# Partial sums of a first half kept in DRAM instead of SBUF, with more buffers for a stream of weights

## The chip, the cores and the metric

One core of a Trainium2 chip runs the whole program. The metric is the device time of one execution in microseconds (us). The kernel before takes 1258.06 us, the median of three runs (1256.82 to 1258.31). The execution that the profiler recorded took 1256.72 us; its instructions span 1254.9 us.

## The reference

Attention with normalised queries and keys, then a layer with squared ReLU, then a gated pair of products:

```python
q_n, k_n = rmsnorm(q, g_q), rmsnorm(k, g_k)          # 4 x 12 heads, 448 x 64
attn = softmax(q_n @ k_n.T / 8);  x = attn @ v       # -> 1792 tokens x 768
r = np.maximum(x @ w_in, 0.0);  x = (r * r) @ w_out  # 768 -> 2048 -> 768
h = (x @ w1) * (x @ w2) @ w3;   y = h @ w_out2       # 768 -> 1024 -> 1024 -> 768
```

The weights come as 64-bit floats, `q`, `k` and `v` as 32-bit ones.

## The kernel before

**Work and batches.** The four batches of 448 tokens follow one another. While the attention of batch b+1 runs head by head (the loop over `h`, lines 663 to 697), the matrix products of batch b fill the gaps of TensorE (PE): `fill(n)` draws pieces of three matmuls from a generator, six times a head. During batch 0 the filler is the product of `w3` and the second `w_out`, formed once (`gen_w3o`, to about 195 us). Then come the products of batch 0 (`gen_moe(0)`, about 195 to 511 us, beside heads 14 to 25), batch 1 (to about 780), batch 2 (to about 1046), and batch 3 with no attention beside it. A product is split in high and low parts, so each block of weights takes three matmuls (L258 to L260).

**The stream of weights.** Weights come in numbered units of 128 x 384 or 128 x 512 numbers. For batch 0 of `w_in`, `w_out`, `w1` and `w2` (88 units) a unit is 64-bit, and its way has many stations: a load by SP's queue into a `raw64` tile (L178); two passes that make 32-bit words in place (L192 on ScalarE, L197 on GpSimd or L195 on ScalarE); a *join* on VectorE (DVE, L204) into a `raw` tile; a store of that to DRAM for the later batches (L212); the high part copied into an `hl` tile (L104, ScalarE) and the low part subtracted into it (L112, mostly GpSimd). For batches 1 to 3 the unit is loaded as 32-bit straight into a `raw` tile (L181). There are 4 `raw64`, 4 `raw` and 4 `hl` tiles. `advance(u)`, called when unit u is used, issues the loads up to u+2+5 (64-bit) or u+2+3 (32-bit), words to u+2+3, joins to u+2+2, the low parts to u+2.

**Tiles of the products.** `relu2` (L324) uses an `r` and a `gf` tile: ReLU, its square, the product of PSUM and `r`, and the low part. The second product of each layer sums over 2048 rows in two halves: `keep` copies the sums of the first half into six `acc` tiles, `add` (L342) adds the second half to them. Results leave through `osb` tiles.

**Attention's last step.** `stage_v` puts the sums of two heads into `xf` (L617, DVE). `stage_x`, called in the next iteration, transposes the norms on PE (L598) into the only tile of the pool `ps_kv`, and DVE multiplies (L623). `stage_k` and `stage_v` use the same PSUM tile.

**What sets the order.** Each engine and each DMA queue works in order. The order is set at build time by a scheduler that follows the program's order, dependences and free tiles.

Of the kernel before, what the change touches and what calls it, by code (L numbers as in the profile page):

```python
# [29 lines left out]
def attention_moe_kernel(  # L30
# [15 lines left out]
    nc = tc.nc  # L46
    B, P, H, C, D = q_nat.shape
# [20 lines left out]
    VLO_ENG = "gvgv"  # L68


    SPLIT_AHEAD = 2
    HI_AHEAD = 1
    JOIN_AHEAD = 2
    WORD_AHEAD = 3
    LOAD32_AHEAD = 3
    LOAD64_AHEAD = 5

    const = ctx.enter_context(tc.tile_pool(name="const", bufs=1))
    xp = ctx.enter_context(tc.tile_pool(name="x", bufs=8))
    actp = ctx.enter_context(tc.tile_pool(name="act", bufs=8))  # L80
    x2p = ctx.enter_context(tc.tile_pool(name="x2", bufs=6))
    accp = ctx.enter_context(tc.tile_pool(name="acc", bufs=6))
    rawp = ctx.enter_context(tc.tile_pool(name="raw", bufs=4))
    hlp = ctx.enter_context(tc.tile_pool(name="hl", bufs=4))
    t2 = ctx.enter_context(tc.tile_pool(name="t2", bufs=2))
    t1 = ctx.enter_context(tc.tile_pool(name="t1", bufs=1))
    t3 = ctx.enter_context(tc.tile_pool(name="t3", bufs=3))
# [4 lines left out]
    ps_kv = ctx.enter_context(tc.tile_pool(name="ps_kv", bufs=1, space=bass.MemoryType.PSUM))  # L92
    ps_mm = ctx.enter_context(tc.tile_pool(name="ps_mm", bufs=3, space=bass.MemoryType.PSUM))

    w3o = dram.tile([2 * NE, 128, 512], F32, name="w3o")

    ident = const.tile([P, P], F32, name="ident")
# [12 lines left out]
    def sub_on(eng, out, in0, in1):  # L110
        e = nc.vector if eng == "v" else nc.gpsimd
        e.tensor_tensor(out=out, in0=in0, in1=in1, op=ALU.subtract)  # L112
# [59 lines left out]
    def load_next():  # L172
        i = pos["load"]
        src = units[i][0]
        n = src.shape[-1]
        if is64(i):
            t = t3.tile([128, 512, 2], U32, name="raw64", tag="raw64", bufs=4)
            nc.sync.dma_start(out=t[:, :n, :], in_=src.bitcast(U32).rearrange("p (n t) -> p n t", t=2))  # L178
        else:
            t = rawp.tile([128, 512], F32, name="raw", tag="raw")  # L180
            nc.sync.dma_start(out=t[:, :n], in_=src)  # L181
        raws[i] = t
        pos["load"] += 1
# [68 lines left out]
    def use(u):  # L252
        advance(u)
        return hls.pop(u).rearrange("p a (k m) -> p a k m", m=128)

    def mm3(ps, w, wk, x, i, n):
        last = n - 1
        nc.tensor.matmul(ps, w[:, 0, wk, :], x[0], start=(i == 0), stop=False)  # L258
        nc.tensor.matmul(ps, w[:, 0, wk, :], x[1], start=False, stop=False)  # L259
        nc.tensor.matmul(ps, w[:, 1, wk, :], x[0], start=False, stop=(i == last))  # L260
# [7 lines left out]
    def gen_w3o():  # L268
        for ic in range(NIC):
            ws = None  # L270
            for half in range(2):
                ps = ps_mm.tile([128, 512], F32, name="mm", tag="mm")
                for jc in range(NIC):
                    if ws is None or jc * 2 // NIC >= len(ws):
                        ws = (ws or []) + [use(w3_at[2 * ic + len(ws or [])])]
                    if ic == 0:
                        advance(wo_at[half, jc])
                        wo[half, jc] = hls.pop(wo_at[half, jc])
                    w = ws[jc * 2 // NIC]
                    mm3(ps[:, :HC], w, jc % (NIC // 2), hl_pair(wo[half, jc], HC), jc, NIC)  # L280
                    yield 3
                o = t2.tile([128, S], F32, name="osb", tag="osb")
                copy_on("a", o[:, :HC], ps[:, :HC])
                k, c = divmod(ic, NIC // 2)
                nc.sync.dma_start(
                    out=w3o.rearrange("(e k) p (c m) -> e k p c m", k=2, m=128)[half * 3:half * 3 + 3, k, :, c, :]
                    .rearrange("e p m -> p e m"),
                    in_=o[:, :HC].rearrange("p (e m) -> p e m", m=128),
                )
# [26 lines left out]
    def gen_moe(b):  # L316
        u = U0 + b * (2 * NFC + 4 * NE + 4 * NJ + 2 * NE)
        x = [xs.pop((b, i)) for i in range(KX)]
        acc = [None] * NE
        x2 = [None] * NE  # L320
        for half in range(2):
            g = []

            def relu2(ps):  # L324
                r = t2.tile([128, S], F32, name="r", tag="r")
                nc.scalar.activation(out=r, in_=ps, func=AF.Relu)
                t = actp.tile([128, 2, S], F32R, name="act", tag="act")
                gf = t2.tile([128, S], F32, name="gf", tag="gf")
                nc.scalar.activation(out=t[:, 0, :], in_=r, func=AF.Square)
                nc.vector.tensor_tensor(out=gf, in0=ps, in1=r, op=ALU.mult)  # L330
                sub_on("g", t[:, 1, :], gf, t[:, 0, :].bitcast(F32))
                g.append(t)

            def keep(e):
                def f(ps):
                    acc[e] = accp.tile([128, S], F32, name="acc", tag="acc")
                    copy_on("a", acc[e], ps)
                return f

            def add(e):  # L340
                def f(ps):
                    nc.vector.tensor_tensor(out=acc[e], in0=ps, in1=acc[e], op=ALU.add)  # L342
                    t = x2p.tile([128, 2, S], F32R, name="x2", tag="x2")
                    copy_on("v", t[:, 0, :], acc[e])
                    sub_on("g", t[:, 1, :], acc[e], t[:, 0, :].bitcast(F32))
                    x2[e] = t
                return f

            yield from products(u, x, KX, [relu2] * (NFC // 2), half == 0)
            u += NFC  # L350
            yield from products(u, g, KF, [(add if half else keep)(e) for e in range(NE)])
            u += 2 * NE
        ab = []
        left = {}

        def gate(ps):
            left["a"] = t2.tile([128, S], F32, name="r", tag="r")
            copy_on("a", left["a"], ps)

        def gated(ps):  # L360
            abf = t2.tile([128, S], F32, name="gf", tag="gf")
            nc.vector.tensor_tensor(out=abf, in0=ps, in1=left.pop("a"), op=ALU.mult)
            t = actp.tile([128, 2, S], F32R, name="act", tag="act")
            copy_on("a", t[:, 0, :], abf)
            sub_on("g", t[:, 1, :], abf, t[:, 0, :].bitcast(F32))
            ab.append(t)

        yield from products(u, x2, NE, [gate, gated] * NJ)
        u += 4 * NJ

        def out(e):
            def f(ps):
                o = t2.tile([128, S], F32, name="osb", tag="osb")
                copy_on("a", o, ps)
                nc.scalar.dma_start(out=out_t[e * 128:(e + 1) * 128, b * S:(b + 1) * S], in_=o)
            return f

        yield from products(u, ab, NIC, [out(e) for e in range(NE)])
# [222 lines left out]
    def stage_v(h):  # L601
        if not (0 <= h < NH):
            return
        d = heads.pop(h)
        vt = d["v"].rearrange("p c a d -> p c (a d)")
        ps = ps_kv.tile([128, 512], F32, name="kv", tag="kv")
        ops = [(vt[:, kc, :], m) for kc in range(4) for m in d["pt"][kc]]
        for n, (w, m) in enumerate(ops):
            nc.tensor.matmul(ps[:, :S], w, m, start=(n == 0), stop=(n == len(ops) - 1))  # L609
        i = h % 2  # L610
        r0, r1 = i * D, (1 - i) * D
        if i == 0:
            xf[0] = t2.tile([128, S], F32, name="xf", tag="xf")
        x = xf[0]
        tmp = t1.tile([128, S], F32, name="vt", tag="vt")
        copy_on("a", tmp[r0:r0 + D, :], ps[r1:r1 + D, :S])
        nc.vector.tensor_tensor(out=x[r0:r0 + D, :], in0=ps[r0:r0 + D, :S], in1=tmp[r0:r0 + D, :], op=ALU.add)  # L617
# [45 lines left out]
    for h in range(NH + 1):  # L663
        n = W3O / ((H + 1) * 6) if h <= H else MOE / (H * 6)
        load_head(h + 3)
        load_v(h + 1)
        if h % GH == 0:
            load_group(h // GH + 1)
        stage_qk(h, 0)
        fill(n)  # L670
        stage_exp(h, 0)
        if h % H != 1:
            stage_x(h - 2)
        stage_t(h - 1, 0)
# [80 lines left out]
```

## Time and profile before

| | |
|---|---|
| median of three runs | 1258.06 us |
| profiled execution | 1256.72 us, span 1254.9 us |
| mean granted clock of PE | 0.984 |
| busy: PE, ScalarE (ACT), GpSimd (POOL), VectorE (DVE) | 94%, 60%, 63%, 55% |
| read from HBM, written | 149.95 MB, 27.53 MB |

Shares are means over the span. The stages differ a lot, so the table says little about where time is lost; the stretches of the section on rows do.

### The profile page before, as it was taken

The numbers are of one execution on the slowest core, as the hardware profiler recorded it, in microseconds if no ns is written. First come the engines' busy times: TensorE is split into PE (matmuls) and PEld (weight loads), VectorE is DVE, ScalarE is ACT, GpSimd is POOL, SyncE is SP. The second block draws the span as 40 slices with busy tenths as digits, with TensorE's granted clock in tenths as the row PEclk, the third lists the DMA queues.
The fourth block names the chain that finished last, engine by engine and source line by source line (L and its number), as shares of the span: only waits on it lengthen the run. The fifth ranks groups of instructions, "written<-read, shape, count | busy, mean of one in ns | idle before, by whom it ended". The sixth has DMA issues, their size and how long they took to land.

```text
span 1254.9 us, 18695 instructions
## 1 busy us (share of the span) xinstructions
PE 1176.6 (94%) x6192; PEld 1063.9 (85%) x6192; DVE 692.6 (55%) x1274; ACT 749.0 (60%) x1595; POOL 788.5 (63%) x770
## 2 busy tenths in 40 slices
PE   3789999798888999999999999999999999999998
PEld 2578888687777889999999998999999999999998
DVE  6699877666668676556557546555664431012100
ACT  5788877776755665665655555655545554443342
POOL 5874427746765555675876664765765656768773
PEclk9899999998998989999999999999999999999999
DMA  7774447866866754433334344333433333433342
GB/s 211 243 222 135 150 143 205 260 199 192 257 171 200 229 154 143 123 111 115 114 92 124 96 130 137 96 105 86 117 89 88 92 106 110 120 104 111 101 122 94
DMA packets 102129, 178.71 MB, mean 142 GB/s; under 512 B 11056, under 2 KB 65552, under 8 KB 102032
## 3 DMA queue, kind: packets, MB, share of 16 engines
q1 hardware_dynamic: 98576, 172.01, 46.9%
q10 hardware_dynamic: 3456, 5.51, 1.2%
q8 instruction: 49, 0.80, 0.3%
q14 instruction: 48, 0.39, 0.1%
HBM read 149.95 MB, written 27.53 MB: 141 GB/s over the span
## 4 chain that ended last, share of the span: by engine, by line
PE 65%; DVE 5%; DMA 4%; POOL 3%; ACT 2%; issue 2%; SPq 0%; POOLq 0%; DVEq 0%; ACTq 0%
PE mm L258 18%; PE mm L259 18%; PE mm L260 18%; PE pt L560 3%; PE kv L609 3%; DMA raw<-w 2%; DVE raw L204 2%; POOL hl L112 2%; PE sc L520 2%; PE sc L521 2%; DMA raw<-w_in 1%; DVE nb L522 1%; PE kv L504 1%; PE kv L598 1%; ACT p L538 0%
## 5 line engine op out<-in xcount | busy, mean ns | idle before, releaser
L112 POOL TENSOR_TENSOR hl<-raw,hl 128x384 fp32r<-128x384 f32 (+1 forms) x395 | 459.3, 1166 | 270.3 <-ACT hl L104 266.8
L104 ACT ACTIVATE hl<-raw 128x384 fp32r<-128x384 f32 (+1 forms) x416 | 234.0, 564 | 147.2 <-PE mm L260 79.3
L259 PE MATMUL mm<-x,hl 128*128 128x448 f32 (+1 forms) x832 | 307.3, 369 | 7.8 <-POOL x L112 7.8
L258 PE MATMUL mm<-x,hl 128*128 128x448 f32 (+1 forms) x832 | 311.9, 375 | 2.8 <-ACT x L104 1.8
L260 PE MATMUL mm<-x,hl 128*128 128x448 f32 (+1 forms) x832 | 306.3, 368 | 2.0 <-POOL hl L112 1.2
L258 PE MATMUL mm<-act,hl 128*128 128x448 f32 (+1 forms) x640 | 239.0, 373 | 0.0
L259 PE MATMUL mm<-act,hl 128*128 128x448 f32 (+1 forms) x640 | 235.7, 368 | 3.0 <-POOL act L112 2.9
L260 PE MATMUL mm<-act,hl 128*128 128x448 f32 (+1 forms) x640 | 234.6, 367 | 1.6 <-DVE hl L112 1.4
L538 ACT ACTIVATE p<-sc,nb,rr 112x448 f32<-112x448 f32 x192 | 137.5, 720 | 82.3 <-DVE nb L523 81.8
L259 PEld LDWEIGHTS mm<-x,hl 128*128 128x128 f32 x832 | 158.9, 191 | 21.7 <-POOL x L112 9.5
L258 PEld LDWEIGHTS mm<-x,hl 128*128 128x128 f32 x832 | 158.8, 191 | 17.4 <-ACT x L104 3.2
L260 PEld LDWEIGHTS mm<-x,hl 128*128 128x128 f32 x832 | 158.7, 191 | 16.3 <-POOL hl L112 2.3
L204 DVE SCALAR_TENSOR_TENSOR raw<-raw 128x384 uint32<-128x384 uint32 (+1 forms) x120 | 94.9, 794 | 77.0 <-POOL hl L112 66.3
L259 PEld LDWEIGHTS mm<-act,hl 128*128 128x128 f32 x640 | 121.9, 191 | 14.2 <-POOL act L112 4.6
L522 DVE TENSOR_REDUCE nb<-sc 112x1 f32<-112x448 f32 x192 | 113.3, 616 | 35.3 <-PE sc L521 34.0
L260 PEld LDWEIGHTS mm<-act,hl 128*128 128x128 f32 x640 | 121.8, 190 | 11.9 <-DVE hl L112 1.8
L112 POOL TENSOR_TENSOR act<-gf,act 128x448 fp32r<-128x448 f32 x96 | 117.5, 1225 | 22.0 <-DVE gf L330 8.5
L258 PEld LDWEIGHTS mm<-act,hl 128*128 128x128 f32 x640 | 122.2, 191 | 9.4
L112 DVE TENSOR_TENSOR ptr<-pt,ptr 128x448 fp32r<-128x448 f32 x144 | 86.8, 618 | 72.2 <-ACT ptr L104 72.0
L560 PE MATMUL pt<-ident,p 112*128 112x112 f32 (+1 forms) x768 | 101.0, 269 | 13.1 <-DVE ptr L112 10.3
L192 ACT ACTIVATE raw<-raw 128x384 f32<-128x384 f32 (+1 forms) x120 | 71.4, 598 | 57.9 <-DMA raw<-w 25.5
L560 PEld LDWEIGHTS pt<-ident,p 112*128 112x128 f32 (+1 forms) x768 | 82.5, 138 | 20.4 <-DVE ptr L112 10.9
(76 smaller groups left out, 1517.5 us busy)
## 6 DMA issues: line engine op xcount, KB each, us to landing
raw<-f_in SPq DMA_DIRECT2D x96, 192.0 KB, 2.4
raw<-f_out SPq DMA_DIRECT2D x72, 256.0 KB, 2.6
raw<-f SPq DMA_DIRECT2D x96, 192.0 KB, 2.4
raw<-w_in SPq DMA_DIRECT2D x32, 384.0 KB, 3.5
raw<-w_out SPq DMA_DIRECT2D x24, 512.0 KB, 4.2
raw<-w SPq DMA_DIRECT2D x32, 384.0 KB, 3.8
raw<-w3o SPq DMA_DIRECT2D x48, 256.0 KB, 2.7
qt<-q_t SPq DMA_DIRECT2D x48, 224.0 KB, 2.8
```

What stands on the lines that cost most here:

```text
L104: nc.scalar.activation(out=out, in_=in_, func=AF.Copy)
L112: e.tensor_tensor(out=out, in0=in0, in1=in1, op=ALU.subtract)
L192: nc.scalar.activation(out=hi, in_=hi, func=AF.Prelu, scale=2.0**-112, alpha=-(2.0**32))
L204: nc.vector.scalar_tensor_tensor(out=f[:, :n].bitcast(U32), in0=t[:, :n, 1], scalar=3, in1=t[:, :n, 0], op0=ALU.logical_shift_left, op1=AL ...
L258: nc.tensor.matmul(ps, w[:, 0, wk, :], x[0], start=(i == 0), stop=False)
L259: nc.tensor.matmul(ps, w[:, 0, wk, :], x[1], start=False, stop=False)
L260: nc.tensor.matmul(ps, w[:, 1, wk, :], x[0], start=False, stop=(i == last))
L520: nc.tensor.matmul(o[j], d["qh"][:, c * P:(c + 1) * P], d["kt"], start=True, stop=False)
L522: nc.vector.tensor_reduce(out=nb[:, j:j + 1], in_=o[j], axis=AX.X, op=ALU.max, negate=True)
L538: nc.scalar.activation(out=p, in_=o[j], func=AF.Exp, scale=d["rq"][:, c:c + 1], bias=nb[:, j:j + 1], accum_out=sm[:, i, c:c + 1],)
L560: nc.tensor.transpose(ps[:kn, c * P:(c + 1) * P], d["p"][c][:, k0:k0 + kn], ident)
L609: nc.tensor.matmul(ps[:, :S], w, m, start=(n == 0), stop=(n == len(ops) - 1))
```

## The change

- The six `acc` tiles go. `keep` copies to an `r` tile and stores it to a DRAM tensor `half0`; `load_kept` loads it back into an `r` tile: for e = 0 and 1 ahead of the second half's product, for e+2 at the end of `add(e)`. These are 24 stores and 24 loads of 224 KB, on SP's queue.
- `r`, `gf` and `osb` share one ring of four `r` tiles (before: two of each). In `relu2` the product is written over `r`, so it follows the square that reads `r`.
- `xf` has one tile in place of two.
- `raw64` has 6 tiles for 4, `raw` 6 for 4, `hl` 5 for 4; loads run up to u+3+7 or u+3+5, joins to u+3+2, low parts to u+3.
- `stage_x` stands one `fill` later in an iteration, behind the transposes and `v_prep` of the head before.

```diff
-    SPLIT_AHEAD = 2
+    SPLIT_AHEAD = 3
-    LOAD32_AHEAD = 3
-    LOAD64_AHEAD = 5
+    LOAD32_AHEAD = 5
+    LOAD64_AHEAD = 7
-    accp = ctx.enter_context(tc.tile_pool(name="acc", bufs=6))
-    rawp = ctx.enter_context(tc.tile_pool(name="raw", bufs=4))
-    hlp = ctx.enter_context(tc.tile_pool(name="hl", bufs=4))
+    rawp = ctx.enter_context(tc.tile_pool(name="raw", bufs=6))
+    hlp = ctx.enter_context(tc.tile_pool(name="hl", bufs=5))
+    half0 = dram.tile([B, NE, 128, S], F32, name="half0")
-            t = t3.tile([128, 512, 2], U32, name="raw64", tag="raw64", bufs=4)
+            t = t3.tile([128, 512, 2], U32, name="raw64", tag="raw64", bufs=6)
+    def row_tile():
+        return t3.tile([128, S], F32, name="r", tag="r", bufs=4)
...
-                gf = t2.tile([128, S], F32, name="gf", tag="gf")
                 nc.scalar.activation(out=t[:, 0, :], in_=r, func=AF.Square)
-                nc.vector.tensor_tensor(out=gf, in0=ps, in1=r, op=ALU.mult)
-                sub_on("g", t[:, 1, :], gf, t[:, 0, :].bitcast(F32))
+                nc.vector.tensor_tensor(out=r, in0=ps, in1=r, op=ALU.mult)
+                sub_on("g", t[:, 1, :], r, t[:, 0, :].bitcast(F32))
...
             def keep(e):
                 def f(ps):
-                    acc[e] = accp.tile([128, S], F32, name="acc", tag="acc")
-                    copy_on("a", acc[e], ps)
+                    r = row_tile()
+                    copy_on("a", r, ps)
+                    nc.sync.dma_start(out=half0[b, e], in_=r)
                 return f
+            def load_kept(e):
+                if e < NE:
+                    kept[e] = row_tile()
+                    nc.sync.dma_start(out=kept[e], in_=half0[b, e])
             def add(e):
                 def f(ps):
-                    nc.vector.tensor_tensor(out=acc[e], in0=ps, in1=acc[e], op=ALU.add)
+                    acc = kept.pop(e)
+                    nc.vector.tensor_tensor(out=acc, in0=ps, in1=acc, op=ALU.add)
...
+                    load_kept(e + 2)
...
+            if half:
+                load_kept(0)
+                load_kept(1)
...
-            xf[0] = t2.tile([128, S], F32, name="xf", tag="xf")
+            xf[0] = t1.tile([128, S], F32, name="xf", tag="xf")
...
-        if h % H != 1:
-            stage_x(h - 2)
         stage_t(h - 1, 0)
...
             v_prep(h)
+        if h % H != 1:
+            stage_x(h - 2)
         fill(n)
```

**What the scheduler makes of it.** SP's queue before, in the products of batch 0, from the last load of the first half's `w_out` (the first row) to the store of the same unit (the last row); numbers tell tiles apart:

```order
L178 DMA raw64_3046<-w_out 128x1024
L212 DMA f_out_108<-raw_2999 128x512
L178 DMA raw64_3073<-w_in 128x768
L212 DMA f_out_108<-raw_3051 128x512
L178 DMA raw64_3119<-w_in 128x768
L212 DMA f_out_108<-raw_3078 128x512
L418 DMA v_3232<-v_in 128x256
L178 DMA raw64_3153<-w_in 128x768
L212 DMA f_out_108<-raw_3124 128x512
L178 DMA raw64_3187<-w_in 128x768
L212 DMA f_out_108<-raw_3158 128x512
```

The same queue after, up to the store of the last such unit; its load and the first one of `w_in` stand just above this piece:

```order
L212 DMA f_out_106<-raw_2923 128x512
L178 DMA raw64_2999<-w_in 128x768
L212 DMA f_out_106<-raw_2979 128x512
L178 DMA raw64_3043<-w_in 128x768
L212 DMA f_out_106<-raw_3004 128x512
L178 DMA raw64_3079<-w_in 128x768
L423 DMA qt_2960<-q_t 128x448
L212 DMA f_out_106<-raw_3048 128x512
L178 DMA raw64_3126<-w_in 128x768
L212 DMA f_out_106<-raw_3084 128x512
L178 DMA raw64_3160<-w_in 128x768
L212 DMA f_out_106<-raw_3131 128x512
```

Before, four loads of `w_in` are issued between a unit's load and its store; after, six (five of them here, one above).

SP's queue after, where the kept sums of batch 0 are loaded back (`r<-half0`), among loads of `w1` and `w2` and stores of `w_out`:

```order
L178 DMA raw64_4075<-w1 128x768
L212 DMA f_out_106<-raw_4039 128x512
L346 DMA r_3911<-half0_99 128x448
L346 DMA r_3913<-half0_99 128x448
L346 DMA r_4032<-half0_99 128x448
L178 DMA raw64_4101<-w2 128x768
L346 DMA r_4072<-half0_99 128x448
L212 DMA f_out_106<-raw_4080 128x512
L431 DMA v_4151<-v_in 128x256
L178 DMA raw64_4164<-w1 128x768
```

Four of the six loads stand together behind the third load of `w1` and `w2`, and each stands behind a load that waits for a `raw64` tile.

DVE before, in the products of batch 0 (the place of rows 4 below), around steps of attention that PE waits for (`xf` is L617 and L623, `ptr` the low parts of the transposed scores, `gf` the squares' product):

```order
L204 SCALAR_TENSOR_TENSOR raw_3631<-raw64_3492 128x384
L108 CAST vhl_3644<-v_3232 128x4x64
L112 TENSOR_TENSOR vhl_3644<-v_3232,vhl_3644 128x4x64
L617 TENSOR_TENSOR xf_3217<-kv_3505,vt_3513 64x448
L522 TENSOR_REDUCE nb_3529<-sc_3530 112x1
L522 TENSOR_REDUCE nb_3529<-sc_3534 112x1
L523 TENSOR_TENSOR nb_3529<-nb_3529,rr_2638 112x2
L330 TENSOR_TENSOR gf_3548<-mm_3472,r_3545 128x448
L112 TENSOR_TENSOR hl_3560<-raw_3497,hl_3560 128x384
L204 SCALAR_TENSOR_TENSOR raw_3655<-raw64_3553 128x384
L623 TENSOR_TENSOR xf_3217<-kv_3576,xf_3217 128x448
L112 TENSOR_TENSOR ptr_3590<-pt_3585,ptr_3590 128x448
```

DVE after, at the same head; the step L617, now L630, stands just above this piece:

```order
L535 TENSOR_REDUCE nb_3537<-sc_3542 112x1
L108 CAST vhl_3641<-v_3240 128x4x64
L536 TENSOR_TENSOR nb_3537<-nb_3537,rr_2646 112x2
L112 TENSOR_TENSOR vhl_3641<-v_3240,vhl_3641 128x4x64
L204 SCALAR_TENSOR_TENSOR raw_3727<-raw64_3560 128x512
L332 TENSOR_TENSOR r_3553<-mm_3480,r_3553 128x448
L112 TENSOR_TENSOR ptr_3588<-pt_3583,ptr_3588 128x448
L112 TENSOR_TENSOR ptr_3595<-pt_3590,ptr_3595 128x448
L204 SCALAR_TENSOR_TENSOR raw_3765<-raw64_3597 128x512
L204 SCALAR_TENSOR_TENSOR raw_3784<-raw64_3623 128x512
L332 TENSOR_TENSOR r_3616<-mm_3559,r_3616 128x448
L636 TENSOR_TENSOR xf_3225<-kv_3644,xf_3225 128x448
```

The step L623 (L636 after) stood behind one join and ahead of the `ptr` rows; now it stands behind three joins, two `ptr` rows and two products of squares. On PE the transposes L598 move with it: before, 8 transposes of scores and 27 matmuls stood between them and those of `stage_k`, which write the same PSUM tile; after, 12 matmuls. Where 4 score matmuls and 15 others stood between `stage_v` and L598, now 4 and 30 and 8 transposes do. From the first products of batch 0 on, the order of all other instructions of PE is the same; in the first 75 us some attention of heads 0 to 2 moves behind matmuls of `gen_w3o`.

## Rows read from the trace of the kernel before

**Rows 1.** The page, engines and TensorE clock in 40 slices of 31.4 us (tenths)
```profile
PE   3789999798888999999999999999999999999998
...
PEclk9899999998998989999999999999999999999999
```

**Rows 2.** Busy us by stretch: PE, PEld, DVE, ACT, POOL, clock, DMA share, GB/s
```profile
40.00:195.00 155.00, 138.61 (x817) 122.91 (x818) 132.23 (x264) 128.67 (x280) 83.00 (x97) 0.98 0.58 175
195.00:450.00 255.00, 221.33 (x1094) 194.37 (x1092) 174.00 (x306) 171.92 (x369) 161.63 (x166) 0.93 0.74 216
...
511.00:780.00 269.00, 268.75 (x1457) 246.25 (x1456) 159.82 (x285) 156.73 (x341) 177.97 (x165) 1.00 0.39 113
...
1046.00:1255.00 209.00, 205.31 (x1016) 190.01 (x1014) 24.15 (x38) 83.32 (x159) 142.30 (x128) 1.00 0.37 108
```

**Rows 3.** Waits of PE, 195 to 450 us: total us, times, longest
```profile
PE kv L598 <- DVE xf L617: 11.9, 4, 4.2
PE pt L560 <- DVE ptr L112: 9.2, 5, 3.5
PE sc L520 <- ACT p L538: 8.8, 8, 2.9
```

**Rows 4.** Timeline of DVE before 304 us: start, duration, instruction, idle before
```profile
297.57 1.36 DVE L204 SCALAR_TENSOR_TENSOR raw<-raw 128x384 uint32<-128x384 uint32 x1 [2.45 <-POOL hl L112]
...
301.90 0.56 DVE L204 SCALAR_TENSOR_TENSOR raw<-raw 128x384 uint32<-128x384 uint32 x1 [1.97 <-POOL hl L112]
...
302.69 0.43 DVE L112 TENSOR_TENSOR vhl<-v,vhl 128x256 fp32r<-128x256 f32 x1
303.15 0.63 DVE L617 TENSOR_TENSOR xf<-kv,vt 64x448 f32<-64x448 f32 x1
```

**Rows 5.** Timeline of PE after it
```profile
303.83 1.01 PE L598 MATMUL kv<-ident,rsw 112*128 112x112 f32 x4 [4.00 <-DVE xf L617]
...
306.91 0.57 PE L260 MATMUL mm<-x,hl 128*128 128x448 f32 x1
...
309.52 0.37 PE L259 MATMUL mm<-x,hl 128*128 128x448 f32 x1
```

**Rows 6.** Busy us by shorter stretches, columns as in rows 2
```profile
225.00:250.00 25.00, 19.10 (x86) 15.31 (x85) 15.17 (x24) 18.66 (x37) 19.45 (x18) 0.93 0.84 268
300.00:345.00 45.00, 36.43 (x177) 32.75 (x178) 30.21 (x49) 32.57 (x69) 32.13 (x31) 0.87 0.80 241
303.90:309.00 5.10, 5.10 (x20) 4.80 (x21) 4.65 (x8) 3.96 (x10) 2.58 (x3) 0.50 0.51 173
```

**Rows 7.** Waits of all engines, 195 to 450 us
```profile
DVE raw L204 <- POOL hl L112: 61.3, 37, 3.3
ACT raw L192 <- DMA raw<-w: 25.5, 18, 4.0
...
ACT raw L192 <- DMA raw<-w_in: 16.0, 13, 2.6
```

**Rows 8.** Waits of SP's DMA queue, 195 to 450 us
```profile
SPq L178 <- DVE raw L204: 139.2, 61, 5.1
```

**Rows 9.** Instructions on raw tiles, 195 to 450 us: count, min/median/max ns; last row: landings
```profile
L204 DVE SCALAR_TENSOR_TENSOR raw<-raw x76: 500/688/1637, 195.2 to 446.7; 128x384 uint32<-128x384 uint32 x52, 128x512 uint32<-128x512 uint32 x24
...
DMA to landing us min/median/max: 3.3/4.0/5.9
```

**Rows 10.** SP's wait for single-precision loads, whole run
```profile
SPq L181 <- POOL hl L112: 585.5, 309, 6.6
```

**Rows 11.** The page, DMA issues: count, KB, median us to landing
```profile
raw<-f_in SPq DMA_DIRECT2D x96, 192.0 KB, 2.4
...
raw<-w_out SPq DMA_DIRECT2D x24, 512.0 KB, 4.2
```

**Rows 12.** Groups of line and form: count, busy us, mean ns, idle before
```profile
L329 ACT ACTIVATE act<-r 128x448 fp32r<-128x448 f32 x64 | 36.7, 574 | 0.0
...
L623 DVE TENSOR_TENSOR xf<-kv,xf 128x448 f32<-128x448 f32 x24 | 14.9, 620 | 9.1 <-PE kv L598 9.1
```

More of the change, by code (lines that the diff above doesn't have):

```diff
@@ L281, in gen_w3o @@
                     yield 3
-                o = t2.tile([128, S], F32, name="osb", tag="osb")
+                o = row_tile()
                 copy_on("a", o[:, :HC], ps[:, :HC])
@@ L318, in gen_moe @@
         x = [xs.pop((b, i)) for i in range(KX)]
-        acc = [None] * NE
         x2 = [None] * NE
+        kept = {}
         for half in range(2):
@@ L324, in relu2 @@
             def relu2(ps):
-                r = t2.tile([128, S], F32, name="r", tag="r")
+                r = row_tile()
                 nc.scalar.activation(out=r, in_=ps, func=AF.Relu)
                 t = actp.tile([128, 2, S], F32R, name="act", tag="act")
-                gf = t2.tile([128, S], F32, name="gf", tag="gf")
                 nc.scalar.activation(out=t[:, 0, :], in_=r, func=AF.Square)
-                nc.vector.tensor_tensor(out=gf, in0=ps, in1=r, op=ALU.mult)
-                sub_on("g", t[:, 1, :], gf, t[:, 0, :].bitcast(F32))
+                nc.vector.tensor_tensor(out=r, in0=ps, in1=r, op=ALU.mult)
+                sub_on("g", t[:, 1, :], r, t[:, 0, :].bitcast(F32))
                 g.append(t)
@@ L335, in f @@
                 def f(ps):
-                    acc[e] = accp.tile([128, S], F32, name="acc", tag="acc")
-                    copy_on("a", acc[e], ps)
-                return f
+                    r = row_tile()
+                    copy_on("a", r, ps)
+                    nc.sync.dma_start(out=half0[b, e], in_=r)
+                return f
+            def load_kept(e):
+                if e < NE:
+                    kept[e] = row_tile()
+                    nc.sync.dma_start(out=kept[e], in_=half0[b, e])
             def add(e):
                 def f(ps):
-                    nc.vector.tensor_tensor(out=acc[e], in0=ps, in1=acc[e], op=ALU.add)
+                    acc = kept.pop(e)
+                    nc.vector.tensor_tensor(out=acc, in0=ps, in1=acc, op=ALU.add)
                     t = x2p.tile([128, 2, S], F32R, name="x2", tag="x2")
-                    copy_on("v", t[:, 0, :], acc[e])
-                    sub_on("g", t[:, 1, :], acc[e], t[:, 0, :].bitcast(F32))
+                    copy_on("v", t[:, 0, :], acc)
+                    sub_on("g", t[:, 1, :], acc, t[:, 0, :].bitcast(F32))
                     x2[e] = t
+                    load_kept(e + 2)
                 return f
@@ L356, in gate @@
         def gate(ps):
-            left["a"] = t2.tile([128, S], F32, name="r", tag="r")
+            left["a"] = row_tile()
             copy_on("a", left["a"], ps)
         def gated(ps):
-            abf = t2.tile([128, S], F32, name="gf", tag="gf")
-            nc.vector.tensor_tensor(out=abf, in0=ps, in1=left.pop("a"), op=ALU.mult)
             t = actp.tile([128, 2, S], F32R, name="act", tag="act")
+            abf = left.pop("a")
+            nc.vector.tensor_tensor(out=abf, in0=ps, in1=abf, op=ALU.mult)
             copy_on("a", t[:, 0, :], abf)
@@ L372, in f @@
             def f(ps):
-                o = t2.tile([128, S], F32, name="osb", tag="osb")
+                o = row_tile()
                 copy_on("a", o, ps)
```

## The prediction

> **What bounds the kernel now.** I read the page's 40 slices first [rows 1]: PE is busy at nine tenths or more and its clock is full in nearly every slice behind 470 us, and both digits fall between about 190 and 450 us. So the stretches follow [rows 2]. Between 511 and 780 us PE is busy 268.75 of 269 us at a clock of 1.00: no wait is left there, and no buffer can gain anything. The same holds with 205.3 of 209 in the last batch. From 195 to 450 us, the products of batch 0, PE is busy 221.3 of 255 us at a mean clock of 0.93. That stretch loses 33.7 us to waits, and (1 - 0.93) x 255 = 17.9 us of clock, most of it while PE works; I take 17. At full clock the same work is 221.3 - 17 = 204 us, so 51 us are lost here. From 40 to 195 us another 16.4 us go to waits.
>
> Who makes PE wait in that stretch is in the waits [rows 3]: steps of attention on DVE and ACT (`xf` 11.9 us, `ptr` 9.2, `p` 8.8), not weights. But the order of instructions on DVE says why these steps are late. The timeline before 304 us [rows 4] shows two joins (L204) that wait 2.45 and 1.97 us for a GpSimd subtraction; behind them in DVE's queue stand `vhl` and L617, done at 303.8 us; and PE, which waited 4.00 us, starts L598 at 303.83 [rows 5]. Then PE's clock is at its half level, 1.2 GHz, from 303.9 to 309 us (granted 0.50) [rows 6], and a matmul takes 0.57 us instead of 0.37 [rows 5]. So an attention wait is a weight wait passed on, and it costs twice.
>
> The weight waits themselves [rows 7, 8]: joins wait 61.3 us for GpSimd to free a `raw` tile, ACT waits 25.5 and 16.0 us for loads, and SP's queue waits 139.2 us of the 255 for a join to free a `raw64` tile. 76 joins run in 255 us [rows 9], one unit per 3.36 us; with four `raw64` tiles a tile takes 4 x 3.36 = 13.4 us from load to load. PE needs only 204 / 76 = 2.68 us per unit. The ring of tiles is what is too slow.
>
> **The change part by part.** All against the profiled execution: a span of 1254.9 us in 1256.7 us; the median of three runs stands 1.3 us above that.
>
> *More tiles and lead.* With six `raw64` tiles and the same 13.4 us a tile, a unit comes every 13.4 / 6 = 2.24 us, below the 2.68 that PE needs. The ring may stretch to 16.1 us before it binds. Landings take 4.0 us at the median and 5.9 at most [rows 9]; were all as slow as that, the ring would be 15.3 us and a unit 2.55. The `raw` ring goes from 4 to 6 in the same way, which gives the join two units, 5.4 us at PE's pace, where its longest wait was 3.3 [rows 7]. So PE should become the bound of the stretch. What is late next: DVE, ACT and GpSimd hold 174, 172 and 162 us of work there [rows 2], near 80, 79 and 74% of the new length, in fixed order, so some waits stay. The nearest rows for what stays are 40 to 195 us, where DVE and ACT are busy 85 and 83% and PE waits 16.4 of 155 us (11%), and 511 to 780 us, where they are busy 59 and 58% and PE waits 0.1%. I take 8%, nearer the first: 204 / 0.92 = 222 us, 33 us less than 255. Short waits cost no clock between 63 and 188 us, where its digit stays 9 [rows 1], so no clock term is added.
>
> *Sums through DRAM.* 24 stores and 24 loads of 224 KB on SP's queue. Of these 12 fall into the stretch, 2.75 MB beside the 55.1 MB (216 GB/s x 255 us) it moves: 5% more, 0.74 to about 0.9 of the DMA engines if all of 58 MB fits into 222 us. A load of this size lands in about 2.4 to 4.2 us [rows 11]. Cover: a product here is 24 matmuls of 205.3 / 1016 = 0.20 us [rows 2], 4.9 us and more beside attention. A load issued by `add` has two products of time, the first two loads one, and two other PSUM accumulators stand behind that. I cost it at nothing; without the cover, see the third rival.
>
> *Squares over their factor.* DVE's product must now wait for the square, 0.574 us [rows 12], 16 times in the stretch: 0 to 9.2 us of DVE's time, 4% of 222. In the last batch three accumulators hide it. Part of the 8%.
>
> *`stage_x` later.* L598 was PE's costliest wait, 11.9 us in four cases [rows 3]. It now has 15 matmuls and 8 transposes more of cover, some 4 us against a longest wait of 4.2. In exchange only 12 matmuls, 12 x 0.2 = 2.4 us, cover the multiplication L623 (0.62 us [rows 12]) before `stage_k` needs the PSUM tile, and on DVE it stands behind `ptr` and joins. Where PE bounds, DVE has that time; in the stretch it can give back 0 to 2 us in each of the four cases. Both are inside the 8%; from 511 us on I cost it at nothing, ten cases of 0 to 0.6 us as the upper end, 6 us.
>
> *The first 75 us.* Matmuls of the filler move ahead of attention. More tiles let loads start earlier, but nothing in the rows says that a shift there gains or loses; I take 0, between -4 and +4 us, a quarter of the 16.4 us that wait there.
>
> Sum: 1256.7 - 33 + 1.3 = 1225 us.
>
> **A rule on DMA against the trace.** The best rates that the stretch shows are 268 GB/s over 25 us and 241 over 45 us [rows 6]; 58 MB take 216 us at the one and 240 at the other, so the transfers stand next to PE as a bound. The Trainium skill's page "DMA: Bandwidth & Descriptors", section "Bandwidth", measured 341 GB/s for transfers of 1 MB on one core and says that smaller ones fall off; by its figure 58 MB would be an estimated 170 us and DMA no bound at all. The trace never comes near that rate, with transfers of 192 to 512 KB, and I go by the trace.
>
> **The rivals.**
> 1. *DMA becomes the bound.* The sustained 241 GB/s is all there is for this mix of loads, stores and sums: the stretch takes 240 us, 15 less, and the run 1243. For it: the share is already 0.80 to 0.84 in these rows. Against: at 268 GB/s it was 0.84, so the engines were not full, and SP was waiting for tiles, not for bandwidth [rows 8].
> 2. *The stream isn't what binds.* The ring's 13.4 us are mostly time in the full queues of POOL, DVE and ACT, and would grow to 20 us with six tiles: the same 3.36 us a unit, no gain, 1258. For it: joins wait for GpSimd rather than for loads [rows 7]. Against: all three engines are idle for a third of the stretch [rows 2].
> 3. *Slower: kept sums come late.* A kept load stands in SP's queue behind weight loads that wait up to 6.6 us for a tile [rows 10] and needs 2.4 more to land [rows 11], 9.0 in all, and DVE's `add` waits in front of everything else on DVE. One product covers 4.9. If each of the 24 adds cost PE the difference, 4.1 us, that is 98 us and a run of 1225 + 98 = 1323; from 33 / 24 = 1.4 us per add on, the kernel is slower than before. For it: each of these loads follows a waiting weight load, and batches 1 to 3 have no slack on PE to pay from. Against: three are issued together, and two accumulators more let PE go on.
>
> **How the numbers follow.** Forecast 0.60, rival 1 0.23, rival 2 0.08, rival 3 0.09. The forecast's own range takes what stays from 3 to 11% of the stretch (210 to 229 us) and the start's 4 us: 1209 to 1236. Up to rival 1 with its 4 us gives 1247; below, nothing but a stretch of PE alone (204 us) lies, 1207. I give 1210 to 1247, which leaves the two last rivals and a little of each end out. 0.2% of this time, 2.5 us, is what a measurement can tell. Faster: the forecast, rival 1 and 0.01 of rival 2, a small gain, 0.84; the same: the rest of rival 2, 0.07; slower: rival 3, 0.09.
>
> **What would show it.** In the profile after: the stretch of batch 0 some 33 us shorter, with PE over 90% busy and the clock near 1.00; DVE's wait at L204 for GpSimd and ACT's at L192 for loads down to a few us each; SP's wait for `raw64` tiles no longer a cause of these; the longest PE waits below 2 us; stretches of batches 1 to 3 unchanged within 2 us each; the DMA share in the stretch above 0.8. Rival 1 would show landings of 5 us and more with ACT waiting at L192 as before; rival 2 the same joins waiting for GpSimd with `raw64` loads landed long before; rival 3 DVE waiting for a load of `half0` at the add, in all four batches. I would be wrong in the mechanism if PE's waits go while the clock or the stretch's length stay, or if the gain comes from before 195 us.

## The result and the profile after

The changed kernel takes **1269.84 us**, the median of four runs (1267.80 to 1271.73), against 1258.18 us (1256.82 to 1258.42) for the kernel before. The ratio is 1.0092 with an interval from 1.0073 to 1.0110: slower by 0.9%, where 1225 us and a gain of 2.6% were forecast. The profiled execution took 1271.73 us; its instructions span 1269.6 us, 14.7 more than before.

The page shows the same picture as [rows 1], a little worse. The kernel after, PE and PE's granted clock in 40 slices of 31.7 us (tenths):

```profile
PE   3789989888888799999999999999999999999998
...
PEclk9789999999898999999999999999999999999999
```

The valley between 190 and 450 us is still there. The windows of the kernel after answer to [rows 2]: busy us of PE, PEld, DVE, ACT and POOL, then clock, DMA share, GB/s.

```profile
40.00:195.00 155.00, 137.77 (x784) 123.04 (x785) 131.81 (x257) 126.80 (x276) 88.79 (x99) 0.93 0.60 178
195.00:450.00 255.00, 216.97 (x1086) 192.78 (x1085) 172.53 (x303) 169.90 (x364) 159.91 (x160) 0.93 0.73 220
511.00:780.00 269.00, 267.23 (x1439) 243.45 (x1440) 165.46 (x285) 154.60 (x336) 175.55 (x164) 1.00 0.41 121
```

From 195 to 450 us PE does 1086 matmuls where it did 1094, at the same clock of 0.93: nothing was gained. From 40 to 195 us it does 784 for 817, and the clock is 0.93 for 0.98. From 511 to 780 us it does 1439 for 1457, now with waits.

Windows at fixed times compare different work, so I cut both traces where the same work stands on PE: at the first transposes of `stage_k` of heads 3, 13, 23, 25 and 47. The kernel before, by these stages:

```profile
65.60:184.52 118.92, 108.55 (x668) 98.05 (x668) 103.65 (x214) 99.48 (x218) 59.11 (x73) 1.00 0.55 163
184.52:455.48 270.96, 237.26 (x1181) 208.62 (x1180) 186.68 (x333) 184.82 (x399) 167.29 (x172) 0.94 0.72 211
...
500.17:992.35 492.18, 491.63 (x2664) 450.37 (x2663) 287.62 (x514) 284.72 (x623) 320.64 (x297) 1.00 0.37 107
```

The kernel after, the same stages:

```profile
66.08:191.40 125.32, 113.20 (x667) 101.86 (x668) 110.53 (x221) 102.37 (x223) 65.01 (x77) 0.96 0.57 164
191.40:463.57 272.17, 234.14 (x1182) 208.72 (x1180) 185.09 (x326) 179.08 (x385) 167.61 (x168) 0.94 0.70 211
...
509.67:1006.67 497.00, 494.13 (x2663) 449.96 (x2662) 291.96 (x514) 286.87 (x629) 319.10 (x296) 1.00 0.40 117
```

Of the 14.7 us, 6.4 come from heads 3 to 13 (118.9 to 125.3), 1.2 from heads 13 to 23, where 33 were to be gained, 1.4 from heads 23 to 25 and 4.8 from heads 25 to 47. The other 0.9 lie at the two ends. Heads 13 to 23 are the place of the forecast's gain: 271.0 before, 272.2 after.

Who waits there is unchanged too. Waits of the kernel after from 195 to 450 us (total us, times, longest), to be read beside [rows 3, 7]:

```profile
DVE raw L204 <- POOL hl L112: 64.3, 38, 4.2
...
ACT raw L192 <- DMA raw<-w: 22.5, 13, 4.2
...
PE sc L533 <- ACT p L551: 16.1, 8, 4.7
...
PE kv L517 <- DVE xf L636: 14.5, 4, 5.3
```

Joins wait 64.3 us for GpSimd where they waited 61.3 with four tiles. PE's longest wait grew from 4.2 to 5.3 us. It is one of four at `stage_k` (L517), which waits for the step that the change moved. The timeline of DVE ahead of another of the four, of 4.58 us, shows why (kernel after: start, duration, instruction, idle before and its releaser):

```profile
318.25 1.16 DVE L112 TENSOR_TENSOR ptr<-pt,ptr 128x448 fp32r<-128x448 f32 x2 [0.50 <-ACT ptr L104]
322.19 2.51 DVE L204 SCALAR_TENSOR_TENSOR raw<-raw 128x512 uint32<-128x512 uint32 x2 [2.78 <-POOL hl L112]
324.62 0.61 DVE L332 TENSOR_TENSOR r<-mm,r 128x448 f32<-128x448 f32 x1
325.16 0.61 DVE L636 TENSOR_TENSOR xf<-kv,xf 128x448 f32<-128x448 f32 x1
```

PE behind it in the same kernel (its last product before the wait ended at 321.2 us):

```profile
325.82 0.73 PE L517 MATMUL kv<-ident_r,khl 112*128 112x112 f32 x4 [4.58 <-DVE xf L636]
...
328.28 0.57 PE L262 MATMUL mm<-x,hl 128*128 128x448 f32 x1
```

Two joins wait 2.78 us for GpSimd, then run 2.51 us; behind them in DVE's queue stands `stage_x`'s product (L636), and PE cannot begin `stage_k` without it. Afterwards a matmul takes 0.57 us, at the half level of the clock (granted 0.50 from 324.0 to 330.6 us). This is the picture of [rows 4, 5] with another victim.

What neither page nor waits say had to be counted from the traces: for each join from 195 to 450 us, how many earlier units had not yet had their low part when it started, and how long its unit lay in tiles.

| | before | after |
|---|---|---|
| joins | 76 | 73 |
| of them with as many units ahead as the `raw` ring has room for | 74 (3 of 4) | 72 (5 of 6) |
| mean time from both words made to join | 6.9 us | 14.9 us |
| mean time from join to high part | 9.7 us | 16.8 us |
| DVE idle ahead of joins (times over 0.3 us) | 66.3 us (39) | 64.5 us (36) |

The `raw64` ring, counted at its loads, is full in the same way: at 76 of 76 loads before and 72 of 72 after, all other tiles hold units that are not yet joined. So both rings are full nearly always, whatever their size. The tiles added were filled by units that lie there longer, 32 us where it was 17.

### The profile page after: what moved, and what is told of

It reads as the page before. It is cut to its first block, busy times and chain, and to the rows that moved or that the text cites. A ratio compares the mean times of both kernels' runs of the same rounds, so it can differ in the third digit from the quotient of the medians.

```text
span 1269.6 us, 18706 instructions
## 1 busy us (share of the span) xinstructions
PE 1181.9 (93%) x6192; PEld 1068.7 (84%) x6192; DVE 700.8 (55%) x1274; ACT 749.9 (59%) x1595; POOL 796.6 (63%) x770
## 4 chain that ended last, share of the span: by engine, by line
PE 70%; DVE 10%; POOL 7%; DMA 5%; issue 4%; ACT 4%; SPq 0%; POOLq 0%; DVEq 0%; ACTq 0%
PE mm L261 19%; PE mm L262 19%; PE mm L263 19%; PE pt L573 4%; PE kv L622 3%; PE sc L533 2%; POOL hl L112 2%; PE sc L534 2%; DVE nb L535 2%; DMA raw<-w_in 2%; DVE raw L204 1%; ACT p L551 1%; POOL raw L197 1%; POOL act L112 1%; DMA raw<-w 1%
## 5 line engine op out<-in xcount | busy, mean ns | idle before, releaser
L262 PEld LDWEIGHTS mm<-act,hl 128*128 128x128 f32 x640 | 123.3, 193 | 16.0 <-POOL act L112 6.6
L261 PEld LDWEIGHTS mm<-act,hl 128*128 128x128 f32 x640 | 123.5, 193 | 11.3 <-DVE r L332 0.8
L263 PEld LDWEIGHTS mm<-act,hl 128*128 128x128 f32 x640 | 122.9, 192 | 10.0
L204 DVE SCALAR_TENSOR_TENSOR raw<-raw 128x384 uint32<-128x384 uint32 (+1 forms) x120 | 87.9, 735 | 77.6 <-POOL hl L112 67.4
L112 POOL TENSOR_TENSOR act<-r,act 128x448 fp32r<-128x448 f32 x96 | 117.7, 1226 | 15.4 <-DVE r L332 11.0
L573 PEld LDWEIGHTS pt<-ident,p 112*128 112x128 f32 (+1 forms) x768 | 82.3, 138 | 25.9 <-DVE ptr L112 14.7
```

The source lines that it names most:

```text
L204: nc.vector.scalar_tensor_tensor(out=f[:, :n].bitcast(U32), in0=t[:, :n, 1], scalar=3, in1=t[:, :n, 0], op0=ALU.logical_shift_left, op1=AL ...
L573: nc.tensor.transpose(ps[:kn, c * P:(c + 1) * P], d["p"][c][:, k0:k0 + kn], ident)
```

## The experiments

**Theories**, lettered as in the expectations. A (order): the rings stand full because their consumer, PE, is late; PE is late because joins, placed early in DVE's order, wait at the edge of the ring with steps of attention behind them. B and C: the rings bound the stretch, and another part of the change took the gain back, the moved `stage_x` (B) or the sums through DRAM (C). Under B and C, undoing parts of the change brings the gain to light; under A only the order of DVE does, with any number of tiles. "Before" is the kernel before, timed on the same chip as each run.

### Parts of the change: x1_stagex_only, x4_dram_only, x2_no_stagex, x3_old_rings

x1 is the kernel before with `stage_x` at its new place alone:

```diff
-        if h % H != 1:
-            stage_x(h - 2)
...
+        if h % H != 1:
+            stage_x(h - 2)
```

> The kernel before with one edit: stage_x one fill later. Theory A (order): what costs in batch 0 is that joins stand ahead of attention on DVE and wait there for tiles that nobody needs yet; moving stage_x only moves the place where PE meets the late DVE, from L598 (11.9 us) to the transposes of stage_k (some 10 to 15 us). Then the time stays within 4 us of 1258. Theory B (stage_x): the new wait of stage_k is what made the changed kernel slow; then this one edit costs 8 to 15 us, 1266 to 1273.

x4 is the kernel before with the sums through DRAM and the squares over their factor, rings and `stage_x` as they were:

```diff
-    accp = ctx.enter_context(tc.tile_pool(name="acc", bufs=6))
+    half0 = dram.tile([B, NE, 128, S], F32, name="half0")
...
-                nc.vector.tensor_tensor(out=gf, in0=ps, in1=r, op=ALU.mult)
+                nc.vector.tensor_tensor(out=r, in0=ps, in1=r, op=ALU.mult)
```

> The kernel before with the sums through DRAM, the shared r tiles and one xf tile alone: old numbers of tiles and lead, stage_x at its old place. Theory A: batches 1 to 3 as before within 2 us, the stretch of batch 0 within 6 us: 1255 to 1264. Theory C (the way through DRAM costs): 5 us or more in batches 1 to 3 and waits of DVE for loads of half0; 1264 to 1270.

x2 is the changed kernel with `stage_x` at its old place (the diff of x1, reversed):

> The changed kernel with stage_x at its old place; more tiles, lead, sums through DRAM and shared tiles stay. Theory A: the rings of tiles are full in both kernels, the two more tiles are filled and joins still wait 50 us or more for GpSimd; 1263 to 1272, no gain in batch 0. Theory B: without the new wait the gain that was forecast shows, 1225 to 1250.

x3 is the changed kernel with the old rings and leads:

```diff
-    SPLIT_AHEAD = 3
-    LOAD32_AHEAD = 5
-    LOAD64_AHEAD = 7
+    SPLIT_AHEAD = 2
+    LOAD32_AHEAD = 3
+    LOAD64_AHEAD = 5
...
-            t = t3.tile([128, 512, 2], U32, name="raw64", tag="raw64", bufs=6)
+            t = t3.tile([128, 512, 2], U32, name="raw64", tag="raw64", bufs=4)
```

> The changed kernel with the old numbers of tiles and lead (raw64 4, raw 4, hl 4; 2, 3 and 5 ahead); sums through DRAM, shared tiles and the later stage_x stay. Theory A: the first 195 us are as before, since more lead is what moved attention there; batches 1 to 3 cost up to 5 us for the sums: 1258 to 1264. Theory C (sums through DRAM cost most of the loss): 1266 to 1272.

| | us | before | ratio | heads 3-13 | 13-23 | 25-47 |
|---|---|---|---|---|---|---|
| before | | | | 118.9 | 271.0 | 492.2 |
| after | 1269.84 | 1258.18 | 1.0092 [1.0073, 1.0110] | 125.3 | 272.2 | 497.0 |
| x1 | 1271.24 | 1256.83 | 1.0106 [1.0085, 1.0126] | 119.1 | 277.0 | 496.1 |
| x4 | 1255.69 | 1257.50 | 0.9987 [0.9978, 0.9997] | 118.9 | 267.7 | 493.5 |
| x2 | 1266.69 | 1256.83 | 1.0074 [1.0057, 1.0092] | 122.9 | 275.6 | 492.5 |
| x3 | 1265.66 | 1256.83 | 1.0069 [1.0051, 1.0087] | 121.6 | 271.1 | 496.4 |

x1 came out at the time of theory B for this run, x2 and x4 at those of A, and x3 between its two ranges. But no part uncovers the forecast's gain in heads 13 to 23, where x4's 3.3 us less is the most. Without the moved `stage_x`, the rings still lose (x2). The sums through DRAM cost nothing (x4). The moved `stage_x` costs 14.4 us by itself, of which 6.0 in heads 13 to 23 and 3.9 in heads 25 to 47; the latter term is there in each kernel with the move (after 4.8, x1 3.9, x3 4.2) and small without it (x2 0.3, x4 1.3). The single effects, +14.4 and -1.8, do not add up to x3's +8.8: every edit makes the scheduler lay the queues anew, so that a few us here or there need not be a property of the edit.

### Fewer tiles: x6_fewer_tiles

```diff
-    LOAD64_AHEAD = 5
+    LOAD64_AHEAD = 4
-            t = t3.tile([128, 512, 2], U32, name="raw64", tag="raw64", bufs=4)
+            t = t3.tile([128, 512, 2], U32, name="raw64", tag="raw64", bufs=3)
```

> The kernel before with three raw64 tiles in place of four, loads up to four units ahead in place of five. If the ring of raw64 tiles binds, as the prediction had it, a unit takes 13.4 / 3 = 4.5 us in place of 3.36, 76 units 85 us more: 1330 or above, at the least 1290. Theory A (the tiles wait full for PE, the joins' places in DVE's order cost): a tile is held for 10 us in place of 13.4, and the time moves by less than 12 us: 1246 to 1270.

It takes 1266.62 us against 1257.50 (1.0068 [1.0052, 1.0083]). But the loss is not where the ring was said to bind. Up to head 13 it is 16.6 us slower (201.1 for 184.5 us, with some 60 matmuls moved from ahead of head 3 to behind it), so in that first part fewer tiles or the shorter lead do cost; heads 13 to 23 take 259.3 us, **11.7 less** than before. The run with three tiles from 195 to 450 us, the window and then joins' waits:

```profile
195.00:450.00 255.00, 226.19 (x1157) 199.64 (x1156) 188.25 (x332) 180.49 (x388) 164.44 (x165) 0.96 0.74 219
```

```profile
DVE raw L204 <- POOL hl L112: 42.1, 32, 3.6
```

Were the ring of `raw64` tiles what limits a unit, three tiles at 13.4 us each would give one per 4.5 us, 57 units in 255 us. It made 75. The time that a unit lies between words and join fell from 6.9 to 3.3 us instead. The ring's 13.4 us were no fixed cost.

### The order on DVE: y2_pin_before, y3_pin_x2, y1_pin_after

Each join gets an ordering edge, without a semaphore, behind the last step of attention on DVE that stands before it in the program: the row maxima times their factor (`nb`), the low part of `ptr`, and the two steps that write `xf`. The joins may no longer be placed ahead of these.

```diff
+    def behind(eng):
+        return tc.issue_after(last[eng]) if eng in last else ExitStack()
...
+        with behind("v"):
             nc.vector.scalar_tensor_tensor(
...
-            nc.vector.tensor_tensor(out=x, in0=norms_to_rows(h), in1=x, op=ALU.mult)
+            mark("v", nc.vector.tensor_tensor(out=x, in0=norms_to_rows(h), in1=x, op=ALU.mult))
```

y2 is the kernel before with these edges, y3 is x2 with them (new rings, DRAM sums, old `stage_x`), y1 the whole changed kernel with them.

> The kernel before, with its old tiles, and each join ordered on DVE behind the last attention step that the program traced ahead of it. Joins run 1 to 3 units later. Theory A: joins were not urgent, so DVE's wait at the join falls from 66 us to under 25, PE's waits in batch 0 from 33 us to under 15, and the time to 1225 to 1245. Rival (weights are late, the rings bind): later joins make weights later still, PE waits for hl tiles, 1258 to 1275.

> The changed kernel with stage_x at its old place and each join ordered behind the last attention step on DVE. Theory A: the order was what cost, so the join's wait falls as in the run with old tiles, from 76 us to about 25, and the stretch of batch 0 from 258 to about 230; with a slightly slower start 1228 to 1242, and the two more tiles are worth less than 8 us either way beside 1233.8 with old tiles. Rival (tiles bind once the order is mended): 1215 to 1225.

> The changed kernel whole, stage_x later too, with one edit: each join ordered behind the last attention step on DVE. Theory A: the stretch of batch 0 falls from 272 us (stage_k of head 13 to that of head 23) to 240 to 250, the rest stays as in the changed kernel: 1238 to 1248. If the tiles were wrong in another way than by the joins' places, over 1255.

| | us | before | ratio | 3-13 | 13-23 | 25-47 | idle ahead of joins |
|---|---|---|---|---|---|---|---|
| y2 | 1233.76 | 1256.83 | 0.9808 [0.9793, 0.9824] | 116.7 | 244.5 | 492.4 | 10.2 us (12) |
| y3 | 1236.71 | 1257.50 | 0.9832 [0.9811, 0.9852] | 120.4 | 244.1 | 492.1 | 0.3 us |
| y1 | 1240.68 | 1259.65 | 0.9852 [0.9836, 0.9869] | 121.2 | 240.3 | 498.8 | 0.0 us |

Heads 13 to 23 of y2 and then of y3, columns as above:

```profile
186.75:431.25 244.50, 227.93 (x1182) 202.73 (x1180) 195.46 (x334) 183.30 (x395) 172.70 (x170) 0.97 0.70 231
```

```profile
191.38:435.44 244.06, 225.48 (x1182) 201.89 (x1181) 201.14 (x338) 184.72 (x399) 178.86 (x172) 0.98 0.74 246
```

This decides for A. With **the old tiles** and another order, heads 13 to 23 fall from 271.0 to 244.5 us, 26.5 of the 33 that the forecast gave to new tiles. All three times lie in the ranges of theory A; PE's waits in y2 fell to 17.2 us from 195 to 450 us, not under 15. New tiles with that order take 244.1: they are worth 0.4 us there. With `stage_x` moved as well it is 240.3, 3.8 less, but 6.7 more in heads 25 to 47. That the move helps in heads 13 to 23 holds with the new tiles only (after 272.2, x2 275.6): with the old ones it costs (x1 277.0, before 271.0; x3 271.1, x4 267.7).

One rival stands beside DVE's order. The edges are on DVE, but the scheduler laid the queues of ScalarE and GpSimd anew with them, while PE's order in these heads is the same but for some 8 of 1180 matmuls. How much of the 26.5 us is theirs was not tried.

### How far it goes: y4_pinw_x2, y7_pin_late, y9_pin_lo

y4 is y3 with the word passes on ScalarE ordered in the same way behind attention's steps there:

```diff
-        nc.scalar.activation(out=hi, in_=hi, func=AF.Prelu, scale=2.0**-112, alpha=-(2.0**32))
+        with behind("a"):
+            nc.scalar.activation(out=hi, in_=hi, func=AF.Prelu, scale=2.0**-112, alpha=-(2.0**32))
```

> As the run before it, with the two word passes on ScalarE also ordered behind the last attention step of ScalarE. Theory A: ScalarE's waits for loads (36 us in batch 0 with joins ordered alone) are the same thing on another engine; they fall under 20 us, and the time falls by 2 to 10 us against the run before it. Rival: ScalarE had slack for these waits; within 2 us of it.

It takes 1241.76 us against 1257.50 (0.9873 [0.9856, 0.9890]), 5 us more than y3, which neither theory had. ScalarE's waits for loads did go from the head of its list; this one stands there in y4, 195 to 450 us:

```profile
ACT p L562 <- DVE nb L547: 45.3, 19, 6.2
```

In y3 the exponential waited 18.1 us for the maxima. The word passes that stood in that time now stand behind it, and ScalarE waits with nothing in hand. That this is what costs the 5 us is not shown: heads 13 to 23 take 245.0 us where y3 takes 244.1, and the largest loss is in heads 3 to 13 (123.2 for 120.4).

y7 is y2 with the edges for units from 24 on only, since y2 lost 4.4 us before head 3 (70.0 for 65.6):

```diff
+        with behind("v") if i >= 24 else ExitStack():
```

> The kernel before with joins ordered behind attention on DVE from unit 24 on only, so that the first 65 us keep their old order (with all joins ordered they took 4.4 us more and had 17 us of half clock in place of 7). If that loss is the joins' order there, 1227 to 1232; if it is chance of the start, 1232 to 1237.

y9 is y7 with GpSimd's low parts ordered behind attention's steps on GpSimd:

```diff
+        with behind("g") if eng == "g" and 24 <= i < U1 else ExitStack():
+            sub_on(eng, t[:, 1, :n], raws.pop(i)[:, :n], t[:, 0, :n].bitcast(F32))
```

> As the run before it, with GpSimd's subtractions of weights also ordered behind its last attention step. In batch 0 DVE still waits 20 us for khl of GpSimd with joins ordered. If these waits reach PE as the joins' did, 2 to 8 us below the run before it; if not, or if PE then waits for hl tiles, from 2 below to 8 above.

**y7 takes 1229.12 us against 1259.65: 0.9763 [0.9748, 0.9778].** It beats both kernels and is the best of all runs. In heads 13 to 23 it has y2's order on every engine and takes 244.2 us. y9 takes 1234.50 (0.9800 [0.9786, 0.9814]), so that edge loses 5.4 us: PE waits 10.5 us for low parts from 195 to 450 us (5.4 in y7). The window of y7, the columns as above:

```profile
195.00:450.00 255.00, 236.38 (x1229) 210.42 (x1228) 199.08 (x331) 189.80 (x409) 182.70 (x183) 0.98 0.72 236
```

Waits of y7 in that window:

```profile
POOL hl L120 <- ACT hl L112: 29.0, 22, 5.6
DVE khl L120 <- POOL khl L114: 20.2, 8, 3.1
ACT raw L200 <- DMA raw<-w: 19.1, 18, 2.6
...
PE kv L607 <- DVE xf L626: 6.3, 4, 2.8
```

DVE's largest wait of before, 61.3 us of joins for GpSimd, is gone from the list, with the same four tiles: the joins of y7 find 0 to 3 units ahead of them (6, 23, 34 and 17 of 80 joins). The `raw64` ring is still full at 74 of 77 loads: it stood full and did not bind. GpSimd is the same engine with the same work as before, but it is asked later. PE's wait for `xf` at the same step falls from 11.9 to 6.3 us, and the clock rises from 0.93 to 0.98, with three waits of PE over 2 us in that window where there were six.

## Why the prediction was wrong

**The step that failed** is "More tiles and lead", in its sentence "The ring of tiles is what is too slow". It took the 13.4 us that a `raw64` tile is held for the time that a unit *needs*, and divided it by six. But 13.4 was read off a full ring, as 4 tiles x 3.36 us, and a full ring gives that product whatever makes it full. After the change it is 6 x 255 / 73 = 21.0 us. That is what the second rival forecast, "20 us with six tiles: the same 3.36 us a unit, no gain", and it was given 8%. (Its time, 1258 us, is 12 short of the measured one, for losses that stand in other terms below.) What could have told the two apart without a run is the landing in [rows 9] beside it: 4.0 us of load, and some 2 us of words and join (0.57, 0.65 and 0.69 us at the median); the other 7 us were time in which the unit lay ready. The table of joins shows just that: 6.9 us from words to join.

**What stands behind the full ring.** The prediction saw in [rows 4, 5] that an attention wait is a join's wait passed on, and this was right. It then took the join's wait for a lack of tiles. It is a matter of who goes first: the scheduler seems to place a join in DVE's order as early as it thinks that a tile will be free: with n tiles there are nearly always n - 1 units ahead (74 of 76, then 72 of 73), and the join always stands at the edge of the ring, waiting for GpSimd with attention behind it. More tiles move the edge and leave the wait. That the order and not the ring is the cause is shown by y2 and y7 (old tiles, another order, -26.5 and -26.8 us in heads 13 to 23) and by y3 (new tiles add 0.4). How the scheduler comes to its placing was not tried; the places are read from the traces.

**"Against: all three engines are idle for a third of the stretch."** This was the argument by which the second rival was set at 8%. The share of idle time said nothing here, on an engine that works in order: 66 of DVE's 81 idle us *were* its joins' wait. (The shares of 222 us beside it are 78, 77 and 73%, not 80, 79 and 74; nothing hangs on that.)

**The clock term** was of the right kind: y7's clock in the stretch is 0.98, and the waits and the clock went together in y2, y3, y1 and y7. The forecast wanted 13% of the stretch (222 for 255 us); the order gives 10% (244 for 271), by another means than the one that was named.

**"The first 75 us"**, taken as 0 with 4 us to either side, stand at +0.5 up to head 3; the loss came right behind, +6.4 in heads 3 to 13, which the sum had no term for: "Short waits cost no clock between 63 and 188 us" held for the kernel before only. About 5 of these are clock (half of 10.2 us, below). The windows of the kernel before, ahead of and behind a wait of 2.73 us at head 3:

```profile
70.00:75.00 5.00, 2.27 (x15) 1.90 (x14) 4.86 (x13) 2.50 (x7) 2.32 (x2) 1.00 0.73 194
75.00:82.00 7.00, 6.62 (x43) 5.50 (x41) 6.84 (x16) 6.49 (x14) 5.46 (x8) 1.00 0.74 235
```

The same place after, with a wait of 2.81 us, and a later one, behind a wait of 2.99 us:

```profile
70.00:75.00 5.00, 2.73 (x15) 2.30 (x14) 4.90 (x11) 2.76 (x7) 4.39 (x5) 0.96 0.54 116
75.00:82.00 7.00, 6.46 (x25) 5.79 (x26) 4.63 (x13) 4.63 (x11) 2.20 (x3) 0.54 0.68 206
...
185.00:190.00 5.00, 3.87 (x17) 3.67 (x18) 4.59 (x11) 4.93 (x12) 1.16 (x2) 0.73 0.46 137
```

PE waits as long at the first place in both kernels, and does 25 matmuls behind it where it did 43. Half clock holds for 10.2 us of heads 3 to 13 after, and for none before; idle time there rises by 1.7.

**"`stage_x` later"** had 6 us as the upper end from 511 us on, and 0 as its value. Measured: 4.8 us in heads 25 to 47, of which PE's idle time is 2.3 (0.55 to 2.87 us) and its busy time 2.5. The idle time is not at `stage_k`, the step whose cover was cut, but ahead of transposes of scores. PE's waits after, 510 to 1007 us:

```profile
PE pt L573 <- DVE ptr L112: 2.5, 2, 1.6
PE kv L611 <- DVE xf L630: 0.4, 2, 0.2
```

The four transposes L611 now often stand alone among products, so there are 55 changes from transposes to products where there were 46 (counted on PE), but each costs 0.02 us at most (below). Where the 2.5 us of busy time come from is not located; that the loss goes with the move is what x1, x3 and y1 show.

**"Sums through DRAM"** at nothing was right (x4: 0.9987), and so was "Squares over their factor". The third rival, kept sums late, did not occur: no wait of DVE for a load of `half0` is on record. The first, DMA as a bound at 241 GB/s, is refuted: y1 moves 245 GB/s over the whole stretch at a share of 0.75, and its heads 13 to 23 are the shortest of all.

**Open.** The start's waits of 2.8 and 3.0 us were not traced to one edit: x2 (rings, no move) loses 4.0 us in heads 3 to 13 and x3 (old rings, move) 2.7. Nor is it settled why the effects of the parts don't add, or what part ScalarE's and GpSimd's new orders have in y2's gain.

## What to carry to other kernels

A ring of buffers that stands full doesn't say that it is too small: tiles x interval is then only the interval again, so compare the time that a tile is *worked on* with the time that it lies ready, and ask who empties the ring. Where an engine works in order, a producer step that runs as far ahead as tiles allow can wait at the ring's edge with urgent work behind it, as here; give it an ordering edge behind that work (here -2.4% with no new buffer) before you give it more room. Try each engine and stretch by itself, as a wait in the trace is not enough to go by: y3's ScalarE waited 35 us for loads, and the edge there cost 5 us; on GpSimd and in the first units it cost 5.4 and 4.4.

## What the runs showed of the hardware

- **Two waits of nearly the same length, two clocks.** PE's wait at head 3 in the kernel before:

```profile
74.66 0.58 PE L560 MATMUL pt<-ident,p 112*128 112x112 f32 x4 [2.73 <-DVE nt L428]
```

  The same wait in the kernel after, and the window of its last 0.9 us:

```profile
75.53 0.98 PE L573 MATMUL pt<-ident,p 112*128 112x112 f32 x4 [2.81 <-DVE nt L442]
```

```profile
74.60:75.50 0.90, 0.00 (x0) 0.00 (x0) 0.90 (x5) 0.00 (x0) 0.12 (x1) 0.53 0.83 328
```

  Before, PE stayed at 2.4 GHz (clock 1.00 from 70 to 82 us). After, it was at 1.2 GHz (0.53) in those last 0.9 us already, so the 0.08 us by which this wait is longer did not decide. The work around the two waits differs; what decided is not shown. But so small a shift went along with some 3 us of loss, and a zero for "moves a little" is no safe term.
- **A late second product behind transposes costs almost nothing.** In the kernel after, PE around a lone set of transposes:

```profile
621.02 0.36 PE L263 MATMUL mm<-x,hl 128*128 128x448 f32 x1
621.23 0.55 PE L611 MATMUL kv<-ident,rsw 112*128 112x112 f32 x4
621.54 0.45 PE L261 MATMUL mm<-x,hl 128*128 128x448 f32 x1
621.83 0.36 PE L262 MATMUL mm<-x,hl 128*128 128x448 f32 x1
622.03 0.37 PE L263 MATMUL mm<-x,hl 128*128 128x448 f32 x1
```

  The second product starts 0.29 us after the first, the third 0.20 after the second; over heads 25 to 47 the mean of the former is 0.287 and that of products among products 0.205. But the first product starts 0.03 us after the last transpose, where transposes follow each other by 0.096. From the product ahead (621.02) to the second one behind (621.83) it is 0.81 us, and at those usual distances it would be 0.79. So a change costs 0.02 us at most, not the 0.08 that the second product alone seems to show.
- **Peaks of DMA are hidden in long windows.** The prediction said that the trace never comes near the 341 GB/s that the Trainium skill's page "DMA: Bandwidth & Descriptors", section "Bandwidth", measured for transfers of 1 MB. In short windows it does, with smaller ones. First the kernel before, in the stretch itself, then y1, with loads of 512 KB and stores of 256 KB:

```profile
240.00:245.00 5.00, 3.17 (x13) 2.22 (x12) 2.74 (x6) 3.17 (x7) 3.57 (x4) 0.92 0.93 327
```

```profile
230.00:240.00 10.00, 10.00 (x57) 9.16 (x56) 7.33 (x9) 10.00 (x24) 9.51 (x9) 1.00 1.00 351
```

  So 241 GB/s was what was asked for, not what could be had.
